# A binding for one set of loads and a wider swap DMA in a Fourier mixer with a feed-forward block

## The chip, the core and the metric

The kernel runs on one core of a Trainium2 chip. A core has a matrix engine (TensorE, PE in the profile, with its weight loads shown as PEld), a vector engine (VectorE, DVE), an activation engine (ScalarE, ACT), a general engine (GpSimd, POOL) and a sync engine (SyncE, SP). Here SP only issues DMAs. The DMAs that SP issues form one queue of the core's 16 DMA engines; those that POOL issues form another. The metric is the time of one execution on the device in microseconds, as a median of runs. A profile is one further execution, recorded by the hardware profiler.

## The reference

Eight sequences of 3008 rows with 256 features go through a Fourier layer and then through a feed-forward block:

```python
X = np.fft.rfft(x, axis=1)
Yr = Xr @ w_r - Xi @ w_i + b_r
Yi = Xr @ w_i + Xi @ w_r + b_i
Yr = np.sign(Yr) * np.maximum(np.abs(Yr) - lam, 0.0)    # Yi the same
y = np.fft.irfft(Y, n=x.shape[1], axis=1)
h = y @ w_in                       # 256 -> 2048
r = np.maximum(h, 0.0)
out = (s * (r * r) + b) @ w_out    # 2048 -> 256
```

## The kernel before

The Fourier transform of a sequence is split into two short transforms, each done as matrix products with small tables. For a batch `b` (a sequence) there are four steps. `s1_units(b)` does the first transform on rows of x, gives u and stores it to DRAM (`ud`, line 707). `fwd_units(b)` (from batch 2 on) or `fwd_unit` (batch 1) does the second transform on rows of u that `load_us` has read back in another order, four loads `us<-ud` per batch (line 716). `mix_units(b)` mixes the features with the weights, thresholds, and does the first inverse transform, which gives v; v goes to DRAM in six stores (`vd<-v`, line 850) and comes back in two loads (`vs<-vd`, line 857). `s4_units(b)` does the last inverse transform and gives y in the tile `yt`. Batch 0 has code of its own, in which all of this stays on the core.

The feed-forward block walks over 48 tiles of up to 512 rows, 16 slots to a tile. In each slot `first_mm` makes 128 of the 2048 hidden features (line 952); ACT applies the ReLU (line 959, tile `rt`) for two slots at a time, DVE or ACT squares (lines 966 and 963, tile `gt`); `second_mms` of the tile before accumulates the outputs (line 1010), which DVE scales into `ost` (line 1020) for the stores to `out`.

The two halves run together: while the feed-forward block of one batch runs, the Fourier units of later batches are put into its slots by `schedule(start, span, units)`. Slot 0 is the first of tile 0. Around the change these calls stand: `mix_units(1)` over slots 24 to 65; `us_loads[2]`, the loads of u of batch 2, over slots 75 to 82; `s4_units(1)` from slot 85 on, and `fwd_units(2)` from slot 90 on. That is the order in which the program is written. Within it a scheduler, which works from an estimate of its own for every operation, settles the order of the instructions of each engine when the kernel is built, and so the order in SP's queue; there a DMA whose input is ready by that estimate may come ahead of one that was written before it. Where the order has to be held, the program says so with `tc.issue_after(ins)`: what is traced inside the block is put behind `ins` in its engine's queue, without waiting for `ins` to be finished.

A mix unit `i` of twelve (line 807) makes a 128 by 2 by 256 tile. DVE adds the shared sum out of PSUM (line 816, into slot `t = ring[:, i % 4]` of one large tile `ring`), and thresholds it with three more operations (lines 821 to 823). Then halves change places between the two 64-row halves and the two columns: four copies of 64 by 256 elements, from `t` to the slot `z = ring[:, 6 + i % 6]`. These copies are "the swap". In batch 1 (`old`) units 0 to 5 are swapped by four DMAs each (line 831) and units 6 to 11 by four DVE copies each (line 833); in batches 2 to 7 units 0 to 9 by DMA and units 10 and 11 by DVE. `inv_unit(i)` (line 841) reads `z`; it is written two steps after the mix unit of its own number, so `inv_unit(2k)` follows `mix_unit(2k + 4)`. Two further orders follow from the slots: `mix_unit(i + 4)` overwrites the slot `t` that the swap of unit `i` reads, and a mix unit, an inverse unit, a sum unit and an s1 unit all take turns on two PSUM banks (`psf`).

`load["act"]` and `load["dve"]` are the program's running account of the two engines; `evac` and `first_mm` read it to choose the engine that empties a bank or squares. POOL's loads of x (line 302) begin when the matmuls of line 703 have read the buffer that they fill.

Of the kernel before, what the change touches and what calls it, by code (L numbers as in the profile page):

```python
# [165 lines left out]
def kernel(  # L166
# [507 lines left out]

    UCH = XCH // 2
    us_loads = {}

    def s1_units(b, more_banks=False):

        old = b == 1  # L680
        rows, n = (96, N2) if old else (P, XH)
        ud = dpool.tile([rows, n, D], F16, name="ud", tag="ud")
        hold = {}
        if old:
            xts[b] = bigpool.tile([P, 2 * DC * CLASSES * L1], F16, name="xt", tag="xt")

        def unit(i):
            c, j = divmod(2 * i, XCH)
            k, ju = divmod(2 * i, UCH)
            if ju == 0:  # L690
                if old and k % 2:
                    w = UCH * D
                    hold["u"] = xts[b][:, k // 2 * w : k // 2 * w + w].rearrange(
                        "p (j d) -> p j d", d=D
                    )
                else:
                    hold["u"] = upool.tile([P, UCH, D], F16, name="u", tag="u")
            ps = any_bank() if more_banks else one_bank()
            rhs = x16[(b, c)][:, j * D : (j + 2) * D]
            if old:  # L700
                nc.tensor.matmul(ps[0:96, :], A_t[0:N1, :], rhs[0:N1], start=True, stop=True)
            else:
                nc.tensor.matmul(ps, A_2, rhs, start=True, stop=True)  # L703
            u = hold["u"]
            evac(u[0:rows, ju : ju + 2, :], ps[0:rows].rearrange("p (j d) -> p j d", j=2), 512)
            if ju == UCH - 2:
                nc.sync.dma_start(out=ud[:, k * UCH : (k + 1) * UCH, :], in_=u[0:rows])
            if i == n // 2 - 1 and old:
                for q in range(4):
                    load_us(q)  # L710

        def load_us(q):
            p, g = (P, 6) if old else (2 * SLOTS, GROUPS // 4)
            uv = ud.rearrange("k n d -> (k n) d").rearrange("(q p) d -> p q d", p=p)
            t = uspool.tile([P, g, D], F16, name="us", tag="us")
            nc.sync.dma_start(out=t[0:p], in_=uv[:, g * q : g * q + g, :])
            us[(b, q)] = t

        us_loads[b] = [lambda q=q: load_us(q) for q in range(4)]
        return [lambda i=i: unit(i) for i in range(n // 2)]  # L720

# [24 lines left out]
    def mix_units(b):  # L746

        old = b == 1
        vd = dpool.tile([NPAIR, P, D], F16, name="vd", tag="vd")
        if not ring:  # L750
            ring.append(bigpool.tile([P, 12, 2, D], F16, name="ring", tag="corr"))
        zt = {}
        hold = {}

        def xf(i):
            w = 3 * DC * P
            i %= 4
            return xts[b][:, w * i : w * i + w].rearrange("p (r c k) -> p r c k", r=3, c=DC)

        def fwd_unit(i):  # L760

            bank = one_bank()
            ps = bank.rearrange("p (r c j k) -> p r c j k", r=2, c=DC, j=2)
            t = us[(b, i // 3)]
            for j in range(2):
                q = (2 * i + j) % 6
                for dc in range(DC):
                    nc.tensor.matmul(
                        ps[:, :, dc, j, :], t[:, q, dc * P : (dc + 1) * P],
                        F_t[:, 2 * i + j, :], start=True, stop=True,  # L770
                    )
            xt = xf(i)
            evac(xt[:, 1:3].rearrange("p r c k -> p (r c k)"), bank, 512)
            nc.vector.tensor_tensor(out=xt[:, 0], in0=xt[:, 1], in1=xt[:, 2], op=ALU.add)
            load["dve"] += 0.25

        def xs_of(h):
            if old:
                return [xf(2 * h + i)[:, 0] for i in range(2)]
            xt = xts[b]  # L780
            at = slice(2 * P * h, 2 * P * h + 2 * P)
            xs = xspool.tile([P, DC, 2 * P], F16, name="xs", tag="xs")
            nc.vector.tensor_tensor(out=xs, in0=xt[:, 0, :, at], in1=xt[:, 1, :, at], op=ALU.add)
            load["dve"] += 0.38
            return [xs[:, :, i * P : (i + 1) * P] for i in range(2)]

        def x_of(i, r):
            if old:
                return xf(i)[:, 1 + r]
            return xts[b][:, r, :, i * P : (i + 1) * P]  # L790

        def sum_unit(h):

            xs = xs_of(h)
            ps = one_bank().rearrange("p (i e) -> p i e", i=2)
            for i in range(2):
                for dc in range(DC):
                    nc.tensor.matmul(  # L798
                        ps[:, i, :], xs[i][:, dc], W_g[:, dc, 2],
                        start=(dc == 0), stop=(dc == DC - 1),  # L800
                    )
            s = mpool.tile([P, 2, D], F32, name="s", tag="m")
            nc.scalar.copy(out=s, in_=ps)
            load["act"] += 0.6
            hold[h] = s

        def mix_unit(i):
            ps = one_bank().rearrange("p (r e) -> p r e", r=2)
            for r in range(2):
                for dc in range(DC):  # L810
                    nc.tensor.matmul(  # L811
                        ps[:, r, :], x_of(i, 1 - r)[:, dc], W_g[:, dc, r],
                        start=(dc == 0), stop=(dc == DC - 1),
                    )
            t, m = ring[0][:, i % 4], ring[0][:, 4 + i % 2]
            nc.vector.tensor_tensor(  # L816
                out=t, in0=ps, in1=hold[i // 2][:, i % 2].unsqueeze(1).to_broadcast([P, 2, D]),
                op=ALU.add,
            )

            nc.vector.tensor_tensor(out=m, in0=t, in1=low, op=ALU.max)  # L821
            nc.vector.tensor_tensor(out=m, in0=m, in1=high, op=ALU.min)  # L822
            nc.vector.tensor_tensor(out=t, in0=t, in1=m, op=ALU.subtract)  # L823
            load["dve"] += 1.75

            z = ring[0][:, 6 + i % 6]
            for j in range(2):
                for r in range(2):
                    o, a = z[64 * r : 64 * r + 64, j], t[64 * j : 64 * j + 64, r]
                    if i < (H // 2 if old else H - 2):  # L830
                        nc.sync.dma_start(out=o, in_=a)
                    else:
                        nc.vector.tensor_copy(out=o, in_=a)
                        load["dve"] += 0.13
            zt[i] = z

        def inv_unit(i):
            ps = one_bank().rearrange("p (j e) -> p j e", j=2)
            z = zt.pop(i)
            for j in range(2):  # L840
                nc.tensor.matmul(  # L841
                    ps[:, j, :], T_t[:, 2 * i + j, :], z[:, j, :], start=True, stop=True
                )
            if i % 2 == 0:
                hold["v"] = vpool.tile([P, 4, D], F16, name="v", tag="v")
            v = hold["v"]
            h = 2 * (i % 2)
            evac(v[:, h : h + 2, :], ps, 512)
            if i % 2 == 1:
                nc.sync.dma_start(  # L850
                    out=vd[2 * i - 2 : 2 * i + 2].rearrange("q p e -> p q e"), in_=v
                )
            if i == H - 1:
                vv = vd.rearrange("q (k n) e -> (q k) n e", n=N2)
                for h in range(2):
                    t = vspool.tile([96, HW, D], F16, name="vs", tag="vs")
                    nc.sync.dma_start(out=t, in_=vv[:, h * HW : (h + 1) * HW, :])
                    vs[(b, h)] = t

        units = []  # L860

        def put(f, i, n):
            if 0 <= i < n:
                units.append(lambda: f(i))

        for h in range(H // 2 + 2 + old):
            k = h - old
            if not old:
                put(sum_unit, h, H // 2)
            for i in range(2):  # L870
                if old:
                    put(fwd_unit, 2 * h + i, H)
                put(mix_unit, 2 * k + i, H)
                put(inv_unit, 2 * k - 4 + i, H)
            if old:
                put(sum_unit, h, H // 2)
            if k == H // 2 - 1:
                units += [lambda: None] * 2
        return units
# [238 lines left out]
```

## Time and profile before

| | |
|---|---|
| median of 3 runs | 846.5 us (846.5, 846.5, 850.94) |
| the profiled execution's own time | 849.39 us |
| its span, first to last instruction | 847.6 us |
| PE busy | 832.4 us, 98% of the span |
| DVE, ACT, POOL busy | 692.2, 647.3 and 58.5 us |
| mean granted TensorE clock | 0.998 |
| `ring<-ring` DMAs (the swaps) | 264, 32 KB each |
| `us<-ud` loads | 28, 384 KB each |
| `vd<-v` stores, `vs<-vd` loads | 42 of 256 KB, 14 of 768 KB |
| DVE copies of the swap, line 833 | 72, mean 221 ns |

The span is the time from the first to the last instruction of the profiled execution; the 1.8 us between it and that execution's own time lie around the program. A busy PE is one that has matmuls in it, not one at its peak rate. A line of the timeline gives the start in microseconds, the time taken, the engine (`SPq` is SP's queue, where the time taken is that of issuing), the line of the kernel, the operation, what it writes and reads, and how many stand together; in square brackets is the time the engine stood idle before it and what ended that. A line of the windows view gives a stretch, its length, the busy time of PE, PEld, DVE, ACT and POOL in it with the number of their instructions, the granted clock as a share of full speed, the busy share of the DMA engines, and GB/s.

### The profile page before, as it was taken

The page shows a single profiled execution, that of the slowest core. Times are in us where ns is not written, and L with a number is a line of the kernel's source. Part 1 is how long each engine was busy: PE and PEld are TensorE (multiplying, and loading weights), DVE is VectorE, ACT ScalarE, POOL GpSimd, SP SyncE. Part 2 cuts the span into 40 slices and gives each one's busy share as a digit, 9 for nine tenths or more (in the row PEclk, how much of TensorE's full clock was granted, in tenths as well). Part 3 has the DMA queues.
Part 4 walks back from the last instruction along what each step waited for, and adds up shares of the span by engine and source line. Part 5 has one row for each costly group of instructions (what it writes and reads, how often), then busy time and mean ns, then how long its engine had stood idle before and what let it go on. Part 6 is the DMA issues. An engine that isn't in the chain of part 4 may idle for free.

```text
span 847.6 us, 17209 instructions
## 1 busy us (share of the span) xinstructions
PE 832.4 (98%) x6726; PEld 597.9 (71%) x6726; DVE 692.2 (82%) x1011; ACT 647.3 (76%) x853; POOL 58.5 (7%) x87
## 2 busy tenths in 40 slices
PE   8999998999999999999999999999999999999998
PEld 6857675767777767766776767766677776766766
DVE  5999995888788888898888888888888878776674
ACT  5988875777887788788887887788777877766663
POOL 4640100000001000000001000000000000000000
PEclk9999999999999999999999999999999999999999
DMA  8965775156543674165722656023640222401111
GB/s 199 184 164 132 200 172 162 37 124 157 154 111 75 157 197 121 59 145 147 188 62 59 166 145 168 32 77 112 162 137 26 61 89 89 113 32 39 38 44 51
DMA packets 109225, 97.18 MB, mean 115 GB/s; under 512 B 10956, under 2 KB 98000, under 8 KB 107800
## 3 DMA queue, kind: packets, MB, share of 16 engines
q1 hardware_dynamic: 102200, 80.08, 32.9%
q0 software_dynamic: 6944, 16.00, 11.2%
q8 instruction: 53, 0.87, 0.4%
q14 instruction: 28, 0.23, 0.1%
HBM read 55.34 MB, written 46.66 MB: 120 GB/s over the span
## 4 chain that ended last, share of the span: by engine, by line
PE 86%; DVE 5%; DMA 3%; ACT 3%; issue 2%; POOL 0%; DVEq 0%; ACTq 0%; SPq 0%; POOLq 0%
PE psa L1010 36%; PE psh L952 35%; PE psf L811 4%; PE psf L897 2%; PE psf L841 2%; PE psf L734 2%; PE psf L798 2%; PE psf L703 2%; ACT rt L959 1%; DVE ring L816 1%; DMA x<-in_x_dram 1%; DVE gt L966 1%; PE psm L528 1%; DMA vd<-v 1%; DMA vs<-vd 1%
## 5 line engine op out<-in xcount | busy, mean ns | idle before, releaser
L959 ACT ACTIVATE rt<-psh 128x1024 f32<-128x1024 f32 (+2 forms) x384 | 387.1, 1009 | 111.3 <-PE psh L952 111.0
L966 DVE TENSOR_TENSOR gt<-rt 128x1024 f16<-128x1024 f32 (+2 forms) x319 | 380.6, 1197 | 103.4 <-ACT rt L959 101.0
L1010 PE MATMUL psa<-w_out_t,gt 128*128 128x256 f16 (+1 forms) x3024 | 455.1, 273 | 0.0
L1010 PEld LDWEIGHTS <-gt 128*128 128x128 f16 (+1 forms) x3024 | 301.3, 101 | 187.2 <-issue 2.0
L952 PE MATMUL psh<-yt,w_in 128*128 128x512 f16 (+1 forms) x1344 | 397.9, 378 | 0.2 <-ACT rt L959 0.2
L952 PEld LDWEIGHTS <-w_in 128*128 128x128 f16 x1536 | 140.8, 98 | 26.2 <-issue 3.5
L1020 DVE SCALAR_TENSOR_TENSOR ost<-psa,s_bc,bias_bc 128x512 f32<-128x512 f32 (+2 forms) x97 | 71.0, 732 | 14.3 <-PE psa L1010 13.3
L963 ACT ACTIVATE gt<-rt 128x1024 f16<-128x1024 f32 (+2 forms) x65 | 68.1, 1048 | 1.7
L248 ACT CAST v<-psf 128x512 f16<-128x512 f32 x83 | 48.1, 580 | 18.4 <-PE psf L841 17.1
L816 DVE TENSOR_TENSOR ring<-psf,s 128x512 f16<-128x512 f32 x84 | 57.4, 683 | 3.9 <-PE psf L811 2.3
L248 ACT CAST yt<-psf 128x480 f16<-128x480 f32 (+2 forms) x72 | 44.1, 623 | 17.2 <-PE psf L897 16.6
L952 PE MATMUL psh<-tail,w_in 128*128 128x512 f16 (+1 forms) x192 | 52.1, 353 | 0.0
L248 ACT CAST u<-psf 128x512 f16<-128x512 f32 (+1 forms) x71 | 41.7, 587 | 11.9 <-PE psf L703 11.8
L811 PE MATMUL psf<-W_g,xt 128*128 128x256 f16 x336 | 50.4, 273 | 0.0
L248 ACT CAST xt<-psf 128x480 f16<-128x480 f32 (+3 forms) x71 | 42.5, 599 | 9.0 <-PE psf L734 8.0
L916 POOL COPY tail<-yt 128x896 f16<-128x896 f16 x6 | 10.0, 1666 | 420.2 <-ACT yt L248 327.1
L821 DVE TENSOR_TENSOR ring<-ring,low 128x512 f16<-128x512 f16 x84 | 35.5, 422 | 2.2
L822 DVE TENSOR_TENSOR ring<-ring,high 128x512 f16<-128x512 f16 x84 | 35.4, 422 | 2.2
L823 DVE TENSOR_TENSOR ring<-ring 128x512 f16<-128x512 f16 x84 | 35.4, 422 | 1.8
L811 PEld LDWEIGHTS <-xt 128*128 128x128 f16 x336 | 32.9, 98 | 3.9
L897 PEld LDWEIGHTS <-vs 96*128 96x128 f16 x448 | 30.2, 98 | 6.5 <-DMA vs<-vd 3.8
L302 POOL DMA_DIRECT2D x<-in_x_dram x36 | 18.7, 528 | 222.9 <-PE psf L703 222.9
(114 smaller groups left out, 541.4 us busy)
## 6 DMA issues: line engine op xcount, KB each, us to landing
out_dram<-ost SPq DMA_DIRECT2D x170, 128.0 KB
us<-ud SPq DMA_DIRECT2D x28, 384.0 KB
vd<-v SPq DMA_DIRECT2D x42, 256.0 KB
vs<-vd SPq DMA_DIRECT2D x14, 768.0 KB
x<-in_x_dram POOLq DMA_DIRECT2D x36, 256.0 KB, 5.1
ud<-u SPq DMA_DIRECT2D x36, 256.0 KB
ring<-ring SPq DMA_DIRECT2D x264, 32.0 KB
out_dram<-ost SPq DMA_DIRECT2D x16, 120.0 KB
```

Of the source, the lines that this page charges most:

```text
L248: return None, nc.scalar.copy(out=dst, in_=src)
L811: nc.tensor.matmul(ps[:, r, :], x_of(i, 1 - r)[:, dc], W_g[:, dc, r], start=(dc == 0), stop=(dc == DC - 1),)
L816: nc.vector.tensor_tensor(out=t, in0=ps, in1=hold[i // 2][:, i % 2].unsqueeze(1).to_broadcast([P, 2, D]), op=ALU.add,)
L821: nc.vector.tensor_tensor(out=m, in0=t, in1=low, op=ALU.max)
L822: nc.vector.tensor_tensor(out=m, in0=m, in1=high, op=ALU.min)
L897: nc.tensor.matmul(ps[:, j * 96 : (j + 1) * 96], vs[(b, h)][:, k, ec * P : (ec + 1) * P], C_t if b == 1 else C_2, start=True, stop=True,)
L952: nc.tensor.matmul(o, w_in_t[dc][:, mc * P : (mc + 1) * P], r, start=(dc == 0), stop=(dc == DC - 1),)
L959: nc.scalar.activation(out=rt[:, :, 0:w], in_=ps[:, :, 0:w], func=AF.Relu)
L963: nc.scalar.activation(out=gt[:, :, 0:w], in_=rt[:, :, 0:w], func=AF.Square)
L966: nc.vector.tensor_tensor(out=gt[:, :, 0:w], in0=rt[:, :, 0:w], in1=rt[:, :, 0:w], op=ALU.mult)
L1010: nc.tensor.matmul(ps[0:size, h, :], gts[(ti, mc // 2)][:, mc % 2, sub * size : (sub + 1) * size], w_out_t[:, mc, :], start=(mc == 0), sto ...
L1020: nc.vector.scalar_tensor_tensor(out=ost[0:size, 0:k], in0=ps[0:size, 0:k], scalar=s_bc[0:size], in1=bias_bc[0:size].unsqueeze(1).to_broad ...
```

## The change

Two things are edited.

The loads of u rows for batch 2 (and for no other batch) are put behind the last load of v rows of batch 1 in SP's queue. To that end `last_vs` keeps the last `vs<-vd` load that was traced, and the four loads stand in an `issue_after` block.

The swap DMAs are widened. An even unit that is swapped by DMA issues nothing; the odd unit after it issues four DMAs that each move the rows of both, 64 rows by two slots by 256 elements. In batch 1 units 0 to 7 are now swapped by DMA, and DVE does four units (8 to 11) where it did six; in later batches it is units 0 to 9 as before. The count of swap DMAs goes from 264 to 136, of 64 KB each; that of the DVE copies from 72 to 64, and `load["dve"]` is charged for eight copies less in batch 1.

```diff
     us_loads = {}
+    last_vs = [None]
...
             t = uspool.tile([P, g, D], F16, name="us", tag="us")
-            nc.sync.dma_start(out=t[0:p], in_=uv[:, g * q : g * q + g, :])
+            if b == 2:
+                with tc.issue_after(last_vs[0].ins):
+                    nc.sync.dma_start(out=t[0:p], in_=uv[:, g * q : g * q + g, :])
+            else:
+                nc.sync.dma_start(out=t[0:p], in_=uv[:, g * q : g * q + g, :])
...
             z = ring[0][:, 6 + i % 6]
+            zt[i] = z
+            by_dma = i < (H - 4 if old else H - 2)
+            if by_dma and i % 2 == 0:
+                return
+            ta, za = i % 4 - 1, 6 + i % 6 - 1
             for j in range(2):
                 for r in range(2):
-                    o, a = z[64 * r : 64 * r + 64, j], t[64 * j : 64 * j + 64, r]
-                    if i < (H // 2 if old else H - 2):
-                        nc.sync.dma_start(out=o, in_=a)
+                    jp, rp = slice(64 * j, 64 * j + 64), slice(64 * r, 64 * r + 64)
+                    if by_dma:
+                        nc.sync.dma_start(
+                            out=ring[0][rp, za : za + 2, j], in_=ring[0][jp, ta : ta + 2, r]
+                        )
                     else:
-                        nc.vector.tensor_copy(out=o, in_=a)
+                        nc.vector.tensor_copy(out=z[rp, j], in_=t[jp, r])
                         load["dve"] += 0.13
-            zt[i] = z
...
-                    nc.sync.dma_start(out=t, in_=vv[:, h * HW : (h + 1) * HW, :])
+                    last_vs[0] = nc.sync.dma_start(out=t, in_=vv[:, h * HW : (h + 1) * HW, :])
```

## The prediction

> **What bounds the kernel now.** I read the page first, then the busy time of each engine in stretches of 8 us, then the chain of waits and the timelines of the two stretches where PE stood idle.
>
> ```profile
> span 847.6 us, 17209 instructions
> PE 832.4 (98%) x6726; PEld 597.9 (71%) x6726; DVE 692.2 (82%) x1011; ACT 647.3 (76%) x853; POOL 58.5 (7%) x87
> ...
> 96.00:104.00 8.00, 6.74 (x52) 5.02 (x51) 7.69 (x20) 6.91 (x11) 0.93 (x2) 1.00 0.94 221
> 128.00:136.00 8.00, 6.16 (x45) 4.05 (x42) 4.65 (x5) 4.75 (x5) 0.00 (x0) 1.00 0.74 200
> 136.00:144.00 8.00, 6.34 (x51) 4.28 (x52) 2.45 (x3) 3.99 (x7) 0.00 (x0) 0.79 0.56 152
> ```
>
> PE is the bound, so only its idle time and its slow time can be won. After 152 us the stretches miss 1.3 us in all before the last 8 us. What is left in the reach of this change is the idle time at 96 to 104 and at 128 to 144, where the clock is low too. The chain of waits passes there through two DMAs, and the timelines of PE, of SP's queue and the windows give the detail:
>
> ```profile
> 125.30 6.53 DMA vd<-v
> 131.89 5.72 DMA vs<-vd
> ...
> 137.66 0.39 PE L897 MATMUL psf<-C_t,vs 96*128 96x96 f16 x5 [3.49 <-DMA vs<-vd]
> ...
> 109.57 0.66 SPq L707 DMA_DIRECT2D ud<-u  x1
> 116.51 0.34 SPq L716 DMA_DIRECT2D us<-ud  x1
> 116.95 0.49 SPq L850 DMA_DIRECT2D vd<-v  x1
> 117.49 1.33 SPq L716 DMA_DIRECT2D us<-ud  x2
> 118.91 1.13 SPq L850 DMA_DIRECT2D vd<-v  x1
> 120.14 5.11 SPq L978 DMA_DIRECT2D out_dram<-ost  x2
> 125.30 1.21 SPq L850 DMA_DIRECT2D vd<-v  x1
> ...
> 139.00:142.60 3.60, 3.60 (x23) 2.17 (x20) 1.16 (x1) 2.25 (x4) 0.00 (x0) 0.53 0.30 100
> ```
>
> PE waits 3.49 us for v of batch 1, and then runs at a granted clock of 0.53 for 3.6 us, 3.6 x 0.47 = 1.7 us more. Behind it: SP stood 6.1 us (110.27 to 116.38) at the first u load, which needs the last `ud` store landed; the fourth v store, whose v was ready at 111.3, stood behind it. Then three u loads (1.15 MB) were in the queue ahead of the last v stores. The last v was ready on ACT at 117.4; its store was issued at 125.30 and landed at 131.84.
>
> **The change part by part.**
>
> *The binding.* No load goes away; four issues (0.34 to 1.13 us each) move behind the two v loads. Past them come three v stores, two output stores and both v loads. The wait for the `ud` store stays in the binding's shadow: that store has landed (116.38) long before. Lower bound of what it wins: the landings in SP's queue, by the trace's semaphore updates, come in the order of issue, and the second and third u loads landed at 127.29 and 128.64, 1.35 us apart; three loads less is 4.0 us, so the last v store lands at 127.8, the v load is issued at once and lands 5.72 us later at 133.6, before PE arrives at 134.16. Upper bound: without the jam the last store is issued at about 119.3, lands in 4 to 6 us, and the v load lands at 129 to 131. Both ends take the whole 3.49 us and leave 0.5 to 5 us to spare; the clock loss goes with it. Term: -3.5 and -1.7.
>
> What is late next: the u loads themselves. By the upper bound they come behind v rows that end at 132 and land 1.3 us apart from 133.3 to 137.2; by the lower at 137.5 to 141.5. PE's first use was at 144.79, 7.1 us behind the first v matmul, of which 1.7 was slow clock; so it comes at about 134.2 + 5.4 = 139.6, and the fourth load's rows some ten units later. Nothing waits. The output stores behind them (132.80 before) land near 139, where they landed at 141. Cost 0.
>
> *DVE copies of units 6 and 7 in batch 1.* Eight copies of 222 ns, 1.8 us of a DVE that is full there:
>
> ```profile
> 97.94 0.92 DVE L833 COPY ring<-ring 64x256 f16<-64x256 f16 x4
> 98.89 1.23 DVE L966 TENSOR_TENSOR gt<-rt 128x1024 f16<-128x1024 f32 x1
> 100.03 0.68 DVE L816 TENSOR_TENSOR ring<-psf,s 128x512 f16<-128x512 f32 x1
> ...
> 100.77 0.38 PE L703 MATMUL psf<-x,A 128*128 128x512 f16 x1 [0.80 <-DVE ring L816]
> ```
>
> Without the 0.92 us the add at 100.03 comes early enough to free PE's bank: -0.8. The next such gap (0.49 us at 104.03) follows unit 8's copies, which stay: 0. In exchange, the pair (6, 7) goes out at about 97 to 98, when POOL's loads fill the DMA engines; a `ud` store issued at 97.44 landed at 107.06. `inv_unit(6)` stood at 107.94, now about 107.1. Cost 0 to 1.3 us (the latter if the pair stands behind the `ud` store issued at 102.36); I take 0.2, as the pair is ready 4 us before that store.
>
> *Wider swaps.* SP loses 128 issues of about 0.59 us (median of the swap rows), 75 us of queue time that PE does not see; it shortens SP's backlog in batch 3, where swaps landed up to 11.6 us after their DVE work. Queued 32 KB swaps landed 0.18 us apart, so a pair of twice that is 0.7 us at the end of a queue. But the even unit's rows now leave with the odd's. So I set the landing of each odd unit's swap before against what the even unit's rows are needed for, the inverse unit 2k and the add of unit 2k+4. Spare time in us: batch 1: 2.2, 4.9, 1.6; batch 2: 2.1, 6.6, 5.1, 6.8, 3.6; batch 3: -2.8, 2.4, 1.1, 0.1, -2.1; batch 4 at least 4; batch 5: 1.0, then over 9; batches 6 and 7 at least 4. Two are negative. The last of batch 3 is SP's backlog (ready at 300.24, issued at 305.99), which the halved issues take away: 0. The first is not backlog:
>
> ```profile
> 269.15 2.51 SPq L831 DMA_DIRECT2D ring<-ring  x4
> ...
> 268.52 1.03 POOL L302 DMA_DIRECT2D x<-in_x_dram  x2 [10.43 <-PE psf L703]
> ...
> 273.74 0.68 DVE L816 TENSOR_TENSOR ring<-psf,s 128x512 f16<-128x512 f32 x1
> ...
> 275.08 0.38 PE L841 MATMUL psf<-ring,T_t 128*128 128x256 f16 x2
> ```
>
> Unit 1 is ready at 268.65, just as two x loads start, and its swap landed at 276.55; unit 0's, before them, at 269.32. The pair lands near 276.4, so the add of unit 4 waits from 273.74; behind it on DVE stand three threshold operations, an output scale and the squares, and `inv_unit(0)` needs the bank that this add frees. PE goes on at 276.4 + 0.7 = 277.1 instead of 275.08: +2.0 (0 if the pair gets past the x loads, 2.8 if all of DVE's wait shows).
>
> What the DMA queues do meanwhile, from 269.2 to 273:
>
> ```profile
> q0 software_dynamic: 128, 0.45, 80.2%
> q1 hardware_dynamic: 70, 0.07, 5.5%
> ```
>
> POOL's queue (q0) has the engines, SP's (q1) next to nothing. [...]
>
> The lower DVE account hands about 1 us of work back to DVE in later choices; DVE is 82% busy: 0 either way, within 0.5 us.
>
> **Sum:** -3.5 - 1.7 - 0.8 + 0.2 + 2.0 = -3.8 us, from 849.39 to 845.6 for the profiled execution. The median before, 846.5, lies 2.9 below that execution. With the whole gain it becomes 842.7; if the median runs had no clock loss, so that 2.1 are to be won, 844.4. I take 843.5.
>
> [...]
>
> **The rivals.**
> A, the forecast (chance 0.50): the stall goes, batch 3 pays for its pair. 841 to 846.5.
> B (0.22): no new wait in batch 3, because the order of SP or the moment of the x loads shifts by the 2 us that it takes. For it: unit 0's swap, issued from 265.58, was out at 269.32, as the x loads began to move. Against it: x loads and mix units both follow PE's order. 846.5 - 5.8 = 840.7.
> C (0.13): the binding does nothing for PE, as something else holds the v rows, such as the output stores ahead of the last v store, or the u rows are late by what the v rows gain. Against it: the landing times above. 846.5, from 845 to 848.
> D, the other side (0.15): the pairs land later than the odd swaps did, everywhere, because four 64 KB DMAs queue behind x loads, stores and each other. Place: the spare times above. The point from which it decides is 1 us later: then batch 1 pays 1, batch 3 8, and the gain of 5.8 is gone; at 2 us batch 1 pays 2.4, batch 3 4.8 + 0.9 + 1.9 + 4.1 and batch 5 1.0, 15 less some 4 us that are the same waits seen twice: 846.5 + 11 - 5.8 = 852. For it: lags of 8 to 11 us in batch 3. Against it: in batches 4 to 7 nearly all lags are 3.7 to 5 us, and SP issues half as much.
>
> **How the numbers follow.** The measurement tells about 0.5% from no change, that is 842.3 and 850.7. Faster: most of B (0.20) and a third of A (0.17). Slower: most of D (0.13). The rest, 0.50, is the same. Range 839 to 851: it leaves out the low end of B and the upper half of D.
>
> **What would show it.** Right: in the chain after, no `vs<-vd` near 134; the `us<-ud` loads of batch 2 after both v loads; no clock under 0.9 near 140; the add of unit 4 in batch 3 ends an idle time of DVE of some 2.5 us, released by `ring<-ring`. Wrong: PE waiting at line 734 for u rows; v loads still issued after 130; waits on `ring<-ring` in batches 4 to 7, which had 4 us and more to spare.

## The result, and the profile after

| | before | after |
|---|---|---|
| median of 18 runs each | 848.98 us (845.49 to 851.48) | 843.91 us (843.02 to 846.21) |
| ratio, 95% interval | | 0.9948 (0.9934 to 0.9961) |
| the profiled execution's own time | 849.39 us | 845.37 us |
| its span | 847.6 us | 843.6 us |

The changed kernel is faster by 0.52%, with an interval of 0.39 to 0.66%. The forecast was 843.5 us. The median of three runs that it started from, 846.5 us, was low: over 18 runs the kernel before takes 848.98, close to its profiled execution.

The first lines of the page of the changed kernel, and, below it, four stretches of its windows view:

```profile
span 843.6 us, 16947 instructions
...
PE 831.5 (99%) x6726; PEld 597.9 (71%) x6726; DVE 692.3 (82%) x1005; ACT 646.9 (77%) x851; POOL 58.4 (7%) x87
```

The windows of the changed kernel (columns as explained above, the third last is the granted clock):

```profile
96.00:104.00 8.00, 8.00 (x63) 6.02 (x62) 7.49 (x15) 6.87 (x11) 1.55 (x3) 1.00 0.89 207
128.00:136.00 8.00, 8.00 (x62) 5.60 (x61) 4.84 (x5) 5.57 (x7) 0.00 (x0) 1.00 0.97 257
136.00:144.00 8.00, 7.98 (x89) 5.99 (x87) 6.46 (x9) 6.59 (x11) 0.00 (x0) 1.00 0.71 181
264.00:272.00 8.00, 6.83 (x50) 4.92 (x49) 4.97 (x10) 6.66 (x9) 0.84 (x2) 1.00 0.76 164
```

The stretch from 128 to 144 us, where PE was busy for 12.50 of 16 us and the clock fell to 0.79, is full now and at full clock. The stretch from 96 to 104 us has its 1.26 us back. A new hole of 1.17 us stands at 264 to 272, in batch 3.

To see where the time went, the two traces are laid side by side by the slots of the feed-forward block: for each of the 768 slots the start of its first matmul of line 952 (963 after), and from that the time between two slots. The stretches in which the two kernels differ, in us:

```
slots         after less before   in the prediction
start to 0         +1.97          not foreseen
48 to 56           -0.82          -0.8   DVE's copies of units 6 and 7
56 to 64           +0.24          +0.2   the pair (6, 7)
64 to 72           -0.14           -
80 to 88           -5.32          -5.2   v rows of batch 1, and the clock
112 to 120         -0.58           0     batch 2
200 to 208         +1.44          +2.0   the pair (0, 1) of batch 3
all others         -0.62           0
slot 0 to the last -5.80          -3.8
```

The 1.97 us at the start lie in batch 0, which the change does not touch. In twelve traces of these kernels slot 0 starts anywhere from 45.16 to 47.83 us, with no order by what was edited. So the stretches are counted from slot 0 on in what follows: 790.45 us before, 784.65 after.

SP's queue and PE's use of the v rows in the changed kernel, from the timeline:

```profile
112.76 4.28 SPq L861 DMA_DIRECT2D vd<-v  x2
118.45 1.31 SPq L989 DMA_DIRECT2D out_dram<-ost  x2
119.86 0.51 SPq L861 DMA_DIRECT2D vd<-v  x1
126.80 0.81 SPq L868 DMA_DIRECT2D vs<-vd  x2
127.71 1.19 SPq L989 DMA_DIRECT2D out_dram<-ost  x2
128.94 7.26 SPq L719 DMA_DIRECT2D us<-ud  x3
...
139.12 0.93 SPq L719 DMA_DIRECT2D us<-ud  x1
```

PE's first use of the v rows of batch 1 in the same timeline:

```profile
135.26 0.38 PE L908 MATMUL psf<-C_t,vs 96*128 96x96 f16 x5
```

The last v store is issued at 119.86 instead of 125.30, the v loads at 126.80 instead of 131.89. By the trace's semaphore updates the first v load landed at 132.46, 2.8 us before PE uses it at 135.26; the bracket with a wait is gone from that matmul. All u loads come after the v loads.

The hole in batch 3 of the changed kernel, first in the chain that ended last (start, time, what):

```profile
264.38 0.52 PE psf L816 x4
265.08 6.47 DMA ring<-ring
271.69 0.27 PE psf L852
```

And the same place in its timeline:

```profile
263.81 1.03 POOL L302 DMA_DIRECT2D x<-in_x_dram  x2 [10.44 <-PE psf L704]
...
264.37 2.79 SPq L841 DMA_DIRECT2D ring<-ring  x4
...
271.69 0.56 PE L852 MATMUL psf<-ring,T_t 128*128 128x256 f16 x2 [1.17 <-DMA ring<-ring]
272.04 0.69 DVE L821 TENSOR_TENSOR ring<-psf,s 128x512 f16<-128x512 f32 x1 [2.93 <-PE psf L852]
```

Units 0 and 1 of batch 3 leave together at 264.37, just after POOL's two x loads of 256 KB began. Their four DMAs landed at 271.32 to 271.92, behind the second x load (271.10). A landing is the last of the sixteen updates that a DMA gives its semaphore in the trace; eleven or twelve of the sixteen had come by 269.45 to 270.08, and the last came 1.8 to 1.9 us later. DVE stood idle for 2.93 us, PE for 1.17. The profile names PE's inverse unit, not the swap, as what ended DVE's wait; the two came within 0.3 us of each other.

### The profile page after: what moved, and what is told of

It reads as the page before. It is cut to its first block, busy times and chain, and to the rows that moved or that the text cites. A ratio compares the mean times of both kernels' runs of the same rounds, so it can differ in the third digit from the quotient of the medians.

```text
span 843.6 us, 16947 instructions
## 1 busy us (share of the span) xinstructions
PE 831.5 (99%) x6726; PEld 597.9 (71%) x6726; DVE 692.3 (82%) x1005; ACT 646.9 (77%) x851; POOL 58.4 (7%) x87
## 4 chain that ended last, share of the span: by engine, by line
PE 90%; DVE 3%; DMA 2%; ACT 2%; issue 1%; POOL 0%; DVEq 0%; SPq 0%; ACTq 0%; POOLq 0%
PE psa L1021 37%; PE psh L963 36%; PE psf L816 4%; PE psf L908 2%; PE psf L852 2%; PE psf L803 2%; PE psf L739 2%; PE psf L704 2%; PE psm L528 1%; DMA x<-in_x_dram 1%; ACT rt L970 1%; DVE gt L977 1%; DMA ring<-ring 1%; DVE ring L821 1%; PE psf L559 0%
## 5 line engine op out<-in xcount | busy, mean ns | idle before, releaser
L248 ACT CAST xt<-psf 128x480 f16<-128x480 f32 (+3 forms) x68 | 40.6, 597 | 10.4 <-PE psf L739 9.1
L852 PE MATMUL psf<-ring,T_t 128*128 128x256 f16 x168 | 32.2, 272 | 1.3 <-DMA ring<-ring 1.2
```

The costliest lines, as they stand in the source:

```text
L248: return None, nc.scalar.copy(out=dst, in_=src)
L852: nc.tensor.matmul(ps[:, j, :], T_t[:, 2 * i + j, :], z[:, j, :], start=True, stop=True)
```

## The experiments

Each was compared with runs of the kernel before on the same chip; the changed kernel's own median comes from another set of runs. Times "from slot 0" are from one trace of each kernel; times of stretches are differences of such traces.

**The binding alone.**

```diff
--- before
+++ e1_bind
-            nc.sync.dma_start(out=t[0:p], in_=uv[:, g * q : g * q + g, :])
+            if b == 2:
+                with tc.issue_after(last_vs[0].ins):
+                    nc.sync.dma_start(out=t[0:p], in_=uv[:, g * q : g * q + g, :])
...
-                    nc.sync.dma_start(out=t, in_=vv[:, h * HW : (h + 1) * HW, :])
+                    last_vs[0] = nc.sync.dma_start(out=t, in_=vv[:, h * HW : (h + 1) * HW, :])
```

> The binding alone: the four loads of u rows of batch 2 stand behind the v loads of batch 1 in SP's queue, every swap is as before. Theory 1 (the terms are separate, and the wait for the v rows is the binding's alone): no wait for vs at the first v matmul, no half clock near 140 us, the matmuls of slot 88 come 5.3 us earlier against slot 80; the waits of 0.8 and 0.5 us near 100 us stay, batch 3 has no new wait; in all 5.0 to 5.5 us less than before in the profile, and about the same in the timed runs. Theory 2 (it was the shorter swap work of batch 1 that brought the v rows earlier, with fewer issues on SP and fewer copies on DVE): 2 us or more of the wait for vs are left here, and e2_first wins most of it.

Median 844.78 us, ratio 0.9959 (0.9945 to 0.9973). From slot 80 to 88: -5.32 us against before, the same as in the full change. At most 0.3 us elsewhere; from slot 0 to the end -5.03. So the whole gain at 134 us is the binding's, and the binding is most of the change. How much it wins differs from one execution to the next: among the timed runs of this comparison with a mean granted clock of 1.000, the kernel before has a median of 846.69 us (8 runs) and the binding alone one of 844.69 (5 runs), 2.0 us apart, where all runs together are 4.96 apart.

**The wider swaps in batch 1 alone, and in batches 2 to 7 alone.** Neither has the binding.

```diff
--- after
+++ e2_first
-            if b == 2:
-                with tc.issue_after(last_vs[0].ins):
...
-            if by_dma and i % 2 == 0:
+            wide = old
+            if by_dma and wide and i % 2 == 0:
```

> Batch 1 alone: its units 0 to 7 swapped in pairs by DMA, units 8 to 11 by DVE; later batches swap each unit by itself, the u loads are not bound. Theory 1: 0.6 us less between slots 48 and 72 (0.8 won at the first wait near 100 us, 0.2 paid for the pair), the wait for vs within 1 us of the 3.5 us of before, half clock after it; in all 0.5 to 1.5 us less. Theory 2: the wait for vs falls below 1.5 us, and the whole is 3 us or more less.

```diff
--- after
+++ e3_later
-            if b == 2:
-                with tc.issue_after(last_vs[0].ins):
...
-            by_dma = i < (H - 4 if old else H - 2)
-            if by_dma and i % 2 == 0:
+            by_dma = i < (H // 2 if old else H - 2)
+            wide = not old
+            if by_dma and wide and i % 2 == 0:
```

> Batches 2 to 7 alone: pairs there, batch 1 swaps as before (six units by DMA singly, six by DVE), the u loads are not bound. Theory 1: the wait for vs stays at 3.5 us; batch 3's first pair makes PE wait 1.2 to 2.0 us for ring, which no later batch does; nothing is won in batch 2, since the 0.6 us won there after the change came from which engine empties which bank (the account of DVE is charged less in batch 1 and not here); so 1 to 2 us more than before. Rival: the 0.6 us of batch 2 and the 0.4 us of batches 4 to 7 come from the halved issues on SP, and show here too: then 0 to 1 us more.

Batch 1 alone: median 848.01 us, ratio 0.9994 (0.9976 to 1.0013). It has the -0.81 and +0.23 us of slots 48 to 64, as in the full change, and batch 2's -0.59. The wait for the v rows is 2.89 us here (shown below), within 1 us of the 3.49 of before: theory 1. But from slot 232 to 240 it has a loss of 3.27 us that was not expected. SP's queue there, in this kernel's timeline:

```profile
304.90 0.56 SPq L717 DMA_DIRECT2D us<-ud  x1
305.57 2.47 SPq L838 DMA_DIRECT2D ring<-ring  x4
```

And PE in the same timeline:

```profile
311.75 0.28 PE L851 MATMUL psf<-ring,T_t 128*128 128x256 f16 x1 [2.79 <-DMA ring<-ring]
```

Here the scheduler put a u load of 384 KB ahead of four swaps of batch 3; the swaps landed at 311.48 to 312.24. In the kernel before, this load was issued at 301.75 and had landed (307.20) ahead of these swaps (309.22 to 310.93), and PE's matmuls did not wait for them (its weight loads did, for 0.2 us). By the order in the queue it looks like the first fault over again: rows that are wanted soon stand behind a u load that is wanted later. But the order explains only a part. By the trace's semaphore updates the u load had landed at 309.67, and 15 of the 16 parts (one an update) of each of these swaps by 309.61 to 310.10; the last part came 1.9 to 2.1 us later, at 311.48 to 312.24. What held it is open. The order was not tried by itself.

Batches 2 to 7 alone: median 850.17 us, ratio 1.0011 (0.9990 to 1.0031). The wait in batch 3 is there (+1.86 us from slot 200 to 208); batch 2's 0.58 us are not. The stretch from slot 80 to 88 was 3.35 us shorter than before, though nothing that stands there was edited; so from slot 0 to the end this trace is 1.26 us shorter than before, where 1 to 2 us more were expected. The first use of the v rows in this kernel's timeline:

```profile
136.12 0.39 PE L907 MATMUL psf<-C_t,vs 96*128 96x96 f16 x5 [1.80 <-DMA vs<-vd]
```

The same in the kernel with batch 1's wider swaps alone, which has the old order of the u loads too:

```profile
136.59 0.58 PE L907 MATMUL psf<-C_t,vs 96*128 96x96 f16 x5 [2.89 <-DMA vs<-vd]
```

The window from 136.00 to 139.50 in the first of the two:

```profile
136.00:139.50 3.50, 3.38 (x38) 2.60 (x39) 1.16 (x1) 2.73 (x5) 0.00 (x0) 1.00 0.55 156
```

And in the second:

```profile
136.00:139.50 3.50, 2.91 (x18) 1.91 (x19) 0.48 (x1) 1.76 (x3) 0.00 (x0) 0.52 0.58 158
```

The wait was 1.80 us in the one execution, and no half clock followed; in the other it was 2.89 us and one did. So 1.7 of the 3.35 us are the wait (3.49 before), 1.7 the clock. Why the v rows came earlier there is not settled.

**The u loads behind the last v store only.** This tells what stands ahead of the v stores from what stands ahead of the v loads. (There are six v stores, not the four of the text below; the binding is to the last of them.)

```diff
--- after
+++ e5_store
-                nc.sync.dma_start(
+                last_vs[0] = nc.sync.dma_start(
...
-                    last_vs[0] = nc.sync.dma_start(out=t, in_=vv[:, h * HW : (h + 1) * HW, :])
+                    nc.sync.dma_start(out=t, in_=vv[:, h * HW : (h + 1) * HW, :])
```

> The changed kernel, except that the u loads of batch 2 are bound behind the last of the four v STORES of batch 1, not behind the v loads. The first two u loads then stand directly behind that store and ahead of both v loads (two u loads of 384 KB, 1.3 us apart where they landed in the kernel before). It leaves SP free of the wait at the head of its queue (the first u load waited 6.1 us for the ud store while the fourth v store stood behind it), and brings back only part of the traffic ahead of the v rows. Theory 1, what counted was the wait at the head of the queue together with the v stores behind the u loads: the v rows come at most 2.6 us later than in the changed kernel, where they had 2.8 us to spare; PE waits 0 to 0.5 us for them, no half clock, and the time is that of the changed kernel within 0.5 us. Theory 2, what counted was any u load ahead of the v loads: PE waits 2 us or more for v rows near 134, and the time is 2 us or more above the changed kernel.

Median 844.19 us, ratio 0.9950 (0.9930 to 0.9970); from slot 0 to the end 0.04 us more than the changed kernel. SP's order:

```profile
119.90 0.50 SPq L861 DMA_DIRECT2D vd<-v  x1
120.49 3.67 SPq L719 DMA_DIRECT2D us<-ud  x2
126.81 0.79 SPq L868 DMA_DIRECT2D vs<-vd  x2
```

Two u loads are ahead of the v loads again, and it costs nothing. The v loads are issued at 126.81, when the last v store has landed, as in the changed kernel; the first landed at 133.62 instead of 132.46, still ahead of its use. So what counted was that the v stores got out: theory 1. Whether it was SP's wait at the head of its queue or the u loads' traffic that held the v stores back, this run does not tell; the binding removes both.

**The x loads held back in batch 3.** x of batch 5 waits for v of batch 3.

```diff
--- after
+++ e7_hold
-            plan.setdefault(s1 - 26, []).append(lambda b=b: emit_load_x(b + 1))
+            plan.setdefault(s1 - 26, []).append(
+                lambda b=b: emit_load_x(b + 1, vs[(3, 1)][0:1, 0, 0:1] if b == 4 else None)
+            )
```

> The changed kernel with one thing added: POOL's six loads of x of batch 5, which before filled the DMA engines while batch 3 was mixed, are held until v rows of batch 3 have landed (a one-element copy on POOL from those rows into each buffer ahead of its loads). SP's order is not touched. Theory 1 (the pair of units 0 and 1 of batch 3 is late because POOL's loads have the engines): that pair lands within 5 us of its DVE work instead of 7 to 9, the waits for ring at the add of unit 4 and at inverse unit 0 go, 1.4 us less at slot 208 than the changed kernel; if x of batch 5 then comes late, PE waits at line 704 after slot 285. Rival (the pair is late because of its size or the store ahead of it): the wait stays.

Median 842.65 us, ratio 0.9930 (0.9910 to 0.9950). From slot 200 to 208 it takes what the kernel before took (0.00); elsewhere it is as the changed kernel. The pair (0, 1) was issued at 264.54 and landed at 267.40 to 269.67, the last part 5.6 us after DVE's work where at most 5 were expected; PE did not wait for it.

**Units 0 and 1 of batch 3 swapped singly.**

```diff
--- after
+++ e4_single
-            if by_dma and i % 2 == 0:
+            wide = not (b == 3 and i < 2)
+            if by_dma and wide and i % 2 == 0:
...
+                    if by_dma and not wide:
+                        nc.sync.dma_start(out=z[rp, j], in_=t[jp, r])
```

> The changed kernel with units 0 and 1 of batch 3 swapped each by its own DMAs, as before; all other units in pairs. My theory, that the two units' rows wait because the even unit's leave only with the odd's, after POOL's x loads have begun: unit 0's rows are out before the x loads fill the engines, as in the kernel before, and PE's wait of 1.2 us near 270.5 goes: -1.4 us from slot 200 to 208, nothing elsewhere. The rival, that SP's queue is late there for another reason, such as the order of the output and v stores of the changed kernel, so that unit 0 alone is as late: 0.

Median 842.65 us, ratio 0.9931 (0.9904 to 0.9958). From slot 200 to 208: -1.44 us against the changed kernel, 0.00 elsewhere. Unit 0's rows landed at 260.48 to 262.41, as the x loads began (261.57); unit 1's landed at 269.32 to 269.87. The window of that stretch with the x loads held back:

```profile
264.00:272.00 8.00, 8.00 (x61) 6.22 (x60) 7.24 (x16) 7.23 (x11) 0.00 (x0) 1.00 0.46 125
```

And with single swaps:

```profile
264.00:272.00 8.00, 8.00 (x60) 6.08 (x59) 7.27 (x14) 6.90 (x11) 0.00 (x0) 1.00 0.72 180
```

Either edit fills the hole. The wait needs both: a pair that leaves late, and x loads that are in the engines by then.

**How many units DVE swaps in batch 1: six, and two.**

```diff
--- after
+++ e6_six
-            by_dma = i < (H - 4 if old else H - 2)
+            by_dma = i < (H // 2 if old else H - 2)
--- after
+++ e8_ten
-            by_dma = i < (H - 4 if old else H - 2)
+            by_dma = i < H - 2
```

> The changed kernel with six units of batch 1 swapped by DVE, as before, and the pairs of units 0 to 5 by one DMA each. My reading: from slot 48 to 64 of the traces it loses what the changed kernel won there, 0.82 - 0.24 = 0.6 us; batch 2's 0.58 us (slots 112 to 120) is lost too, as DVE's account is that of before. Sum +1.2 us to the changed kernel, batch 3's wait of 1.4 us unchanged. The rival, that batch 2's 0.58 us come from the pairs: only +0.6 us.

> The changed kernel with ten units of batch 1 swapped by DMA, like the other batches, so that DVE swaps two. My reading: PE's remaining wait of 0.57 us for DVE near 105.6 goes, and DVE has 1.8 us less to do there, but the pair of units 8 and 9 leaves SP amid x loads and ud stores, which landed 4 to 9.6 us after their issue, and inverse unit 8 comes some 4 us behind unit 9: -0.6 to +3 us against the changed kernel, most likely +0.5. The rival, that DVE bounds this stretch and the rows come in time: -0.6 us or better.

Six: median 846.21 us, ratio 0.9970 (0.9948 to 0.9992). Slots 48 to 56 +0.82, 56 to 64 -0.24, batch 2 +0.59, as expected; another 1.0 us went in small steps up to slot 512, which was not: 0.60 of it from slot 400 to 512. From slot 0 to the end +2.13 against the changed kernel.

Two: median 846.59 us, ratio 0.9980 (0.9958 to 1.0001). Slots 48 to 56 -0.53, as DVE is freed, and then 56 to 64 +1.45. PE in the timeline of this kernel:

```profile
113.39 0.28 PE L852 MATMUL psf<-ring,T_t 128*128 128x256 f16 x1 [1.52 <-DMA ring<-ring]
```

The pair (8, 9) landed too late for inverse unit 8. With batch 2's 0.58 us lost as well it is +2.04 from slot 0, more than the +0.5 taken as likeliest, within the range given. Four units on DVE is the best of the three. But about 1.2 of the 2 us in each of the other two lie in batch 2 and from slot 400 to 512, where no swap of batch 1 stands; the next experiment shows whose they are.

**DVE's account charged for the two units it no longer works.**

```diff
--- after
+++ e9_account
+            if old and b == 1 and i == 7:
+                load["dve"] += 1.04
```

> The changed kernel, in which the planner's account charges DVE the 1.04 us for units 6 and 7 of batch 1 that it no longer works (eight copies of 0.13). Nothing else is edited. My reading, that batch 2's 0.58 us come from the account, which hands an operation of that stretch to another engine: the wait of 0.47 us near 178 is back, +0.5 us to the changed kernel, and batch 1 is as in the changed kernel. The rival, that it comes from the two units' lighter work itself or from the order of SP's queue: 0.

Median 844.56 us, ratio 0.9946 (0.9928 to 0.9965). From slot 0 to the end 0.65 us more than the changed kernel. Half of the reading held: batch 2's wait of 0.47 us is back. In the kernel before it was this one:

```profile
177.84 0.38 PE L703 MATMUL psf<-x,A 128*128 128x512 f16 x1 [0.47 <-DVE ring L816]
```

With the charge:

```profile
172.54 0.38 PE L704 MATMUL psf<-x,A 128*128 128x512 f16 x1 [0.47 <-DVE ring L821]
```

The small steps from slot 400 to 512 are lost too, 0.60 us as with six units. The other half of the reading did not hold: batch 1 gained 0.74 us. DVE's timeline in the changed kernel tells why:

```profile
102.25 0.42 DVE L828 TENSOR_TENSOR ring<-ring 128x512 f16<-128x512 f16 x1
102.59 1.22 DVE L977 TENSOR_TENSOR gt<-rt 128x1024 f16<-128x1024 f32 x1
103.72 0.92 DVE L845 COPY ring<-ring 64x256 f16<-64x256 f16 x4
```

The same place with the charge:

```profile
101.69 0.43 DVE L828 TENSOR_TENSOR ring<-ring 128x512 f16<-128x512 f16 x1
102.15 0.93 DVE L845 COPY ring<-ring 64x256 f16<-64x256 f16 x4
103.11 0.29 DVE L779 TENSOR_TENSOR xt<-xt 128x256 f16<-128x256 f16 x1
```

In the changed kernel the planner saw a lighter DVE and gave it a square of 1.22 us in the very stretch that the change had relieved. That square is what PE still waits for there, as the changed kernel's timeline has it:

```profile
105.62 0.38 PE L704 MATMUL psf<-x,A 128*128 128x512 f16 x1 [0.57 <-DVE ring L821]
```

**A version that takes both.** The x loads held back, and the charge put on at unit 7 and taken off at unit 11, so that only the choices between the two differ from those of the changed kernel.

```diff
--- e7_hold
+++ e10_both
-            load["dve"] += 1.75
+            load["dve"] += 1.75 + {(1, 7): 1.04, (1, 11): -1.04}.get((b, i), 0)
```

> The changed kernel with two further edits: the x load of batch 5 held behind the v rows of batch 3, and a charge of 1.04 us to DVE's account at unit 7 of batch 1, taken back at unit 11, so that one gelu product of that stretch (1.22 us at 102.59 in the changed kernel) goes to ACT and the planner's choices after it are as in the changed kernel. If the two are independent: -1.44 us from slot 200 to 208, -0.74 us from slot 48 to 64, batch 2's gain kept; -2.2 us from slot 0 to the end against the changed kernel, about 841.8 us as a median. If the charge only moves the wait (ACT late for the product, as it is 83 to 94% busy there): -1.4 us, 842.6.

(The "gelu product" of the text above is the square of line 977; this kernel has no gelu.) Median 842.13 us, ratio 0.9921 (0.9898 to 0.9945); from slot 0 to the end -2.11 us against the changed kernel, with -0.74 from slot 48 to 64 and -1.44 from 200 to 208. The two are independent, and the windows of the stretches spoken of are full:

```profile
96.00:104.00 8.00, 8.00 (x61) 5.83 (x59) 7.38 (x16) 7.49 (x12) 1.55 (x3) 1.00 0.93 196
104.00:112.00 8.00, 8.00 (x60) 6.24 (x59) 7.81 (x15) 6.39 (x11) 1.03 (x2) 1.00 0.87 231
...
264.00:272.00 8.00, 8.00 (x59) 5.84 (x57) 6.91 (x14) 6.90 (x11) 0.00 (x0) 1.00 0.55 160
```

Its interval overlaps that of the changed kernel, so by the medians alone the 1.8 us between the two are not certain; the slots show them.

## Why the prediction was right, and where it was not

**The binding** (-3.5 and -1.7). Right in place, size and cause. -5.32 us from slot 80 to 88, in the full change and with the binding alone. The bounds had the v rows 0.5 to 5 us ahead of PE; they came 2.8 ahead. The prediction named two causes, SP's wait at its head and the traffic ahead of the last v stores. With the u loads behind the v stores only, nothing is lost: it matters that they stand behind the v stores, not behind the v loads. Which of the two causes weighed more, no run separates.

**The u loads, "nothing waits".** Right, by little. They landed at 139.31, 140.65, 142.19 and 145.85; that is at or past the late end given (137.5 to 141.5, plus 1.26 us by which this execution was late), because output stores came between. PE's first use was at 140.77, 1.5 us after the first landed.

**DVE's copies** (-0.8) and **the pair (6, 7)** (+0.2): -0.82 and +0.24. That the next gap (0.49 us, now 0.57) would stay was right by luck, for another reason: the square that the lower account brought stands in front of it as well as unit 8's copies. Charged back, it went, and the +0.24 with it.

**The pair (0, 1) of batch 3** (+2.0): the wait came where and why it was said to come; +1.44 in size. The rows' arrival was as forecast: 276.4 on the clock of the kernel before is 271.7 here, as this execution was 4.72 us ahead at slot 200, and they landed at 271.32 to 271.92. What was mis-sized is what follows: the prediction let inverse unit 0 wait for the add of unit 4 too, 0.7 us, to free a bank. In the run PE took up the inverse unit at 271.69, as the rows landed, and the add came behind, at 272.04. Without the 0.7 us the forecast is 1.3. That the pair would not get past the x loads was right: its first DMA landed 0.2 us behind POOL's second load (271.32 against 271.10), and with these loads held back the four landed 2 to 4 us earlier. But it was not held whole: eleven or twelve of the sixteen parts of each DMA had landed 1.0 to 1.7 us ahead of that load. In the changed kernel POOL's queue had 51.3% of the 16 engines' time from 265.5 to 270.5 us and SP's 36.2%. What held the last parts back, no run shows; measured is that these 64 KB DMAs, in the engines together with two loads of 256 KB, came 1.17 us too late for PE.

**The other spare times, and the last unit of batch 3.** No other pair made PE wait. The -2.1 us of the last unit of batch 3 were SP's backlog, as said, and went (slots 232 to 240: -0.12). Rival D, pairs late everywhere, fell with that. Rival B, no wait in batch 3, fell with the 1.17 us; C with the binding's own run.

**"The lower DVE account: 0 either way, within 0.5."** The step that failed. The account decides which engine squares, and 23 of the 384 squares, counted in order of time, are on another engine with it. The kernels whose account in batch 1 is that of before (the binding alone, batches 2 to 7 alone, six units, the charge) have the same squares on the same engines as the kernel before; the others, but for two units and the last version, have those of the changed kernel. The lower account cost 0.74 us in batch 1 (the charge took that back) and won 0.58 in batch 2, 0.60 from slot 400 to 512 and some 0.2 in smaller steps: 0.65 us won in all, as the charge shows. That is a little more than the 0.5 allowed, and it is the sum of parts of up to 0.74 us with both signs. With two units on DVE, whose account is lighter still, both gains are lost again. So it is an accident of the planner's choices, not a trend.

**The sum and the time.** From slot 0 on the change won 5.80 us where the sum said 3.8: 0.56 too much for batch 3, 0.58 missed in batch 2, 0.9 of smaller differences, of which 0.6 are the account's from slot 400 to 512. The profiled execution's 845.37 against 845.6 agrees only because its start was 1.97 us late, which is luck. The forecast of 843.5 came near 843.91 by luck too, from a base 2.5 us low with a gain 2.1 us low. The sum of -3.8 against 848.98 would have given 845.2.

**The clock** was the open point between 842.7 and 844.4. Among 60 runs of the kernel before, made along with the first eight experiments, the mean granted clock was at 0.999 or 1.0 in 14 and below in 46; after, it was at 0.999 or 1.0 in 12 of 18. At 1.0 exactly the medians are 846.64 (12 runs) and 843.44 (10 runs), 3.2 us apart, where all runs together are 5.07 apart. So most runs of the kernel before had a lowered clock for some of their time, and not all; where in the run it fell, only a profile shows. By this comparison nearly 2 us of the median gain go with the clock, though runs at full clock may also have had a shorter wait for v, as one trace had (1.80 us). The sum gave 2.1 us for runs without the loss; 3.2 were measured. Two of the three runs that the forecast began from, both at 846.5, lie by their time with those at full clock.

## What to carry to other kernels

Ask of each DMA that waits at the head of a queue who is queued behind it and how soon that is needed. Here SP stood 6.1 us at the first u load with the fourth v store behind it, and four loads that were wanted later cost 5.3 us in the profiled execution. Binding them behind the urgent stores was enough. When one DMA carries the data of two steps, the earlier step's data leaves with the later's: set its landing against the earlier step's need, and look whether another queue's large loads begin in between. And when work is taken off an engine whose account a planner keeps, look at what the planner puts into the room before counting the room as won.

## What the runs showed of the hardware that was not expected

The half clock came for 3.41 us at a time: from 139.09 to 142.51 us in the kernel before, from 15.36 to 18.78 in the changed one. PE had not been idle for all of the 3.41 us before these two: it was busy for 1.43 and 1.46 us of them by the profile. (The ends of matmuls are modelled in a profile, so these two are not exact.) The length of a wait alone did not tell whether half clock followed. A wait of 1.80 us for v (batches 2 to 7 alone) was followed by full clock; one of 1.77 us for x at the start of the changed kernel, with two of 0.18 and 0.20 us shortly before it, by half clock. So a wait can cost more than itself: where the wait for v was 2.89 us (batch 1's wider swaps alone), half clock for 3.41 us made it about 2.89 + 1.7 = 4.6.

The start of the kernel, up to slot 0, varied by 2.7 us over twelve traces (45.16 to 47.83), with waits for x (1.77 us in the changed kernel, 1.68 with the x loads of batch 5 held back) and, in some of them, with half clock. In the changed kernel that began at 15.36 us; with the x loads held back the granted clock was 0.77 from 10 to 14 us and 0.66 from 14 to 18. Between the changed kernel and that with single swaps in batch 3 it is 2.2 us, more than the edit's own 1.44, and it has to be taken out before traces are compared.
